# Weight loads that convert, bfloat16 transposes of the gating matrix, x^T by DMA, and work moved from VectorE to GpSimd and ScalarE in a sparse-attention + gMLP kernel

## Chip, cores and metric

The kernel runs on one core of a Trainium2 chip. The metric is device time in microseconds (us), the median of several executions. Engines are named as in the profile: PE (TensorE matmul), PEld (its weight loads), DVE (VectorE), ACT (ScalarE), POOL (GpSimd), SP (SyncE, which here only issues DMAs).

## What is computed

Four batches, 8 heads, 768 positions, head size 64. Attention where each query looks only into the 6 chunks of 32 keys with the highest upper bound of its score; the result, as x (768×512 per batch), goes through a gated feed-forward block whose gate mixes positions with a 768×768 matrix `w_sg`.

```python
ub = sum(maximum(q * k_min_of_chunk, q * k_max_of_chunk))     # per query and chunk
scores = where(chunk among top 6 and causal, q @ k.T / 8, -1e9)
x = softmax(scores) @ v
u, vv = split(gelu(x @ w_in))                  # w_in 512 x 1024
v_n = (vv - mean(vv)) / sqrt(var(vv) + 1e-6) * g_ln
out = x + (u * (w_sg @ v_n + b_sg)) @ w_out    # w_out 512 x 512
```

Everything arrives and leaves in float32; the matmuls run in bfloat16 except the transposes of q and k and the bound.

## The kernel before

The 32 (batch, head) combinations are handled as 16 pairs of heads, two heads side by side on the 128 partitions; pairs 4b to 4b+3 make batch b. For a pair:

- `loads` and `load_v` bring k, q and v (rows of 64 float32) into one of three buffers each;
- `kside` transposes k on PE in float32 in two halves, takes minimum and maximum of each chunk on DVE (`W`, L519), copies k^T to `KA` in bfloat16, and subtracts the minima from the maxima (L538: the bound is q·min + relu(q)·(max − min));
- `qside` transposes q, evicts it to `qT`, makes relu(q) = `rT` (L556) and casts q to `QA` on POOL (L560); `vside` casts v to `vx` on POOL (L570);
- `select` (pairs 0 to 3) or `select_full` (two pairs together) forms the bounds on PE (L595, L642), transposes them on DVE, finds the sixth largest with MAX8, and makes the 0/1 mask `Dt`; from pair 4 on it is copied by DMA into spare rows of `QA`, so that the mask is added by the score matmul itself;
- `scores` / `scores_full` make scores (L750 and L756, or L710), ACT takes the exponential into `E` (L765, L716; two buffers, so pair p waits until pair p−2 has used its own), and POOL zeroes the upper triangle of the diagonal blocks (L721, L772);
- `head` does attention·V (L788, and L795 for the diagonal blocks), divides by the sum (L803, L805) and puts x into `XS`.

When a pair is done, `xtrans` transposes its 128 columns of x (one block, 128×768) on PE into `xT` (L817) and ACT evicts it (L420, called by `evac`). After four pairs `moe_h` computes the v half (L832), gelu and mean and variance on ACT and DVE (L836, L841, L843), the reciprocal root on POOL (L847), the normalised `vhat` on DVE (L859), then the u half (L870, L875). `moe_g` multiplies `w_sg^T` with `vhat` (L887), scales and gates on DVE (L893, L897), multiplies with `w_out` (L906), adds x (L913) and stores (L917; three buffers `osb`).

The weights are loaded once, by SP, in float32 into places that are free early (`vgb`, `osb`, `xT`, `uT`, `vhat`). POOL casts `w_in` and `w_out` to bfloat16 (`cast`, L416). `w_sg` is transposed on PE in float32, three blocks of 128 columns at a time (L457), and evicted to `wsgT` in bfloat16 by DVE (L423).

The program is a list of operations with their dependences; the order on each engine and the buffer of each PSUM tile come from a table found by a search outside the kernel (`TABLE`). Each engine runs its list strictly in order and waits on semaphores. SP's list is its DMA queue: an entry that waits holds everything behind it. A few warm-up matmuls ("filler", L362) are placed on PE at the start. A class of POOL and ACT operations that move data to other partitions is kept in order on POOL (`shift`).

Of the kernel before, what the change touches and what calls it, by code (L numbers as in the profile page):

```python
# [44 lines left out]
class Program:  # L45
# [215 lines left out]
def _build(nc, ctx, q, k, v, w_in, g_ln, w_sg, b_sg, w_out, out):  # L261
    B, H, S, DH = q.shape
    DM = H * DH
# [50 lines left out]
    KBIG = 16  # L314
    VHACT = ()
# [5 lines left out]
    VACT = 16  # L321
    KDVE = (2,)
    QDVE = (2, 3)
    QACT = 16
    WEV = "dve"
# [3 lines left out]
    vn = [T(f"vn{i}", [128, NT, 2, DH], F32) for i in range(NQS)]  # L329
# [57 lines left out]
    P.op("dve", lambda d: d.tensor_tensor(INDF[:], IND[:, 0], IND[:, 1], op=ALU.add), dve(S, rate=2), ("init", 13),  # L387
         port=True, reads=["IND"] + [("IND", n) for n in range(3)], writes=["INDF"])
# [37 lines left out]
    vgA = vgb[:].rearrange("p a b -> p (a b)")  # L426
    xT1 = xT[1][:].rearrange("p a b -> p (a b)").bitcast(F32)
    uT1 = uT[1][:].rearrange("p a b -> p (a b)").bitcast(F32)
    vh1 = vhat[1][:].rearrange("p a b -> p (a b)").bitcast(F32)
    xT1n = [("xT", 1, dk) for dk in range(NDK)]  # L430
    uT1n = [("uT", 1, fb, tg) for fb in range(NF) for tg in range(2)]
    vh1n = [("vhat", 1, qt) for qt in range(NT)]

    def win_load(i):
        dst = vgA[:, DFF * i:DFF * i + DFF] if i < 3 else xT1[:, 0:DFF]
        names = [("vg", 2 * i), ("vg", 2 * i + 1)] if i < 3 else xT1n
        load(dst, bass.AP(w_in.tensor, 128 * DFF * i, [[DFF, 128], [1, DFF]]), ("wi", i), names, 1700)
        cast(winb[:, i, :], dst, DFF, ("wic", i), names, [("winb", i)])

    def wout_load(j):  # L440
        dst = osb[j][:] if j < 3 else xT1[:, DFF:DFF + DM]
        names = [("osb", j)] if j < 3 else xT1n
        load(dst, bass.AP(w_out.tensor, 128 * DM * j, [[DM, 128], [1, DM]]), ("wo", j), names, 900)
        cast(woutb[:, j, :], dst, DM, ("woc", j), names, [("woutb", j)])

    def wsg_load(j):
        base, names = ((uT1, uT1n), (vh1, vh1n))[j % 4 // 2]
        k2 = j % 2
        dst = base[:, S * k2:S * k2 + S]
        load(dst, bass.AP(w_sg.tensor, 128 * S * j, [[S, 128], [1, S]]), ("ws", j), [("stg", j % 4)], 1350)  # L450
        for hf in range(2):
            t = ps_g.tile((0, 1))

            def tr(e, t=t, dst=dst, hf=hf):
                for x in range(3):
                    c = TG * hf + 128 * x
                    r = e.matmul(t.ap()[:, 128 * x:128 * x + 128], dst[:, c:c + 128], identF[:], is_transpose=True)  # L457
                return r
            P.op("pe", tr, pe32(*[128] * 3), ("wst", j, hf), reads=[("stg", j % 4)] + names + ["identF"], writes=[t],
                 alloc=t)  # L460
            evac(WEV, lambda j=j, hf=hf: wsgT[:, 3 * hf:3 * hf + 3, 128 * j:128 * j + 128],
                 lambda t=t: t.ap()[:, 0:TG].rearrange("p (j x) -> p j x", x=128), TG, ("wev", j, hf), [t],
                 [("wsgT", j, hf)], [t], 1)
# [16 lines left out]
    def load_v(p):  # L480
        s = p % NQS
        for i in range(2):
            P.op("sp", lambda e, i=i: e.dma_start(
                vn[s][:, :, i, :], bass.AP(v.tensor, (2 * p + i) * S * DH,
                                           [[DH, 128], [128 * DH, NT], [1, DH]])), dmac(),
                ("vn", p, i), writes=[("vn", s, i)], dma=f"vn{s}_{i}", xfer=940, bulk=NBULK)
# [9 lines left out]
    def kside(p):  # L496
        s, w = p % NQS, p % NW
        if p < KBIG:
            parts = [(hf, hf + 1, ps_g.tile((0, 1, 2, 3) if p < 6 else (0, 1))) for hf in range(2)]
        else:  # L500
            parts = [(0, 2, [ps_g.tile((x,)) for x in range(2)])]
        for h0, h1, t in parts:
            ts = t if h1 - h0 == 2 else [t]
# [27 lines left out]
        if p >= KSPR:  # L531
# [6 lines left out]
        P.op("dve", lambda d: d.tensor_tensor(W[w][:, 1, 0:NC], W[w][:, 1, 0:NC], W[w][:, 0, 0:NC],  # L538
                                              op=ALU.subtract), dve(24), ("wsub", p), port=True, reads=ws, writes=ws)

    def qside(p):
        s, w, r = p % NQS, p % NW, p % NR
        for hf in range(2):
# [5 lines left out]
            if p >= QACT:  # L549
                for i in range(2) if p >= HALF else (None,):  # L550
                    r0, r1 = (0, 128) if i is None else (64 * i, 64 * i + 64)
                    P.op("act", lambda e, t=t, hf=hf, i=i, r0=r0, r1=r1: e.activation(
                        QA[w][i or 0][r0:r1, TG * hf:TG * hf + TG], t.ap()[r0:r1, 0:TG], ACTF.Copy),
                        act(TG), ("qcast", p), reads=[t], writes=[("QA", w, i or 0, hf)], ps=[t])
        qk = [("qT", r, 0), ("qT", r, 1)]
        P.op("dve", lambda d: d.tensor_scalar(rT[r][:], qT[r][:, LO:S], 0.0, None, op0=ALU.max),  # L556
             dve(NSEL, rate=2), ("rel", p), port=True, reads=qk, writes=[("rT", r)])
        for i in () if p >= QACT else range(2) if p >= HALF else (None,):
# [4 lines left out]
    def vside(p):  # L563
        s, w = p % NQS, p % NW
        rd = [("vn", s, 0), ("vn", s, 1)]
        if p >= VACT:
            P.op("act", lambda e: e.activation(vx[w][:, :, :, 0:DH], vn[s][:], ACTF.Copy), act(S), ("vcast", p),
                 reads=rd, writes=[("vx", w)])
        else:
            P.op("pool", lambda g: g.tensor_copy(vx[w][:, :, :, 0:DH], vn[s][:]), gps(S), ("vcast", p),  # L570
                 reads=rd, writes=[("vx", w)])
# [238 lines left out]
    def xtrans(b, dk):  # L810
        src = XS[:, b % 2, dk]
        rd = [("XS", b % 2, 2 * dk), ("XS", b % 2, 2 * dk + 1)]
        t = ps_g.tile((0, 1))
# [9 lines left out]
    def moe_h(b):  # L823
# [25 lines left out]
        if b in VHACT:  # L849
            P.op("dve", lambda d: d.scalar_tensor_tensor(nmr[s][:], mv[s][:, :, 0], -1.0, rstd[s][:], op0=ALU.mult,  # L850
                                                         op1=ALU.mult), (80, 155), ("nmr", b), port=True,
                 reads=[("rstd", s)] + [("mv", s, qt) for qt in range(NT)], writes=[("nmr", s)])
            for qt in range(NT):
                P.op("act", lambda e, qt=qt: e.activation(vhat[s][:, qt, :], vg[qt], ACTF.Identity,
                                                          bias=nmr[s][:, qt:qt + 1], scale=rstd[s][:, qt:qt + 1]),
                     (F / 1.2 + 110, F / 1.2 + 210), ("vhat", b, qt),
                     reads=[("vg", qt), ("nmr", s), ("rstd", s)], writes=[("vhat", s, qt)])
        for qt in range(NT) if b not in VHACT else ():
            P.op("dve", lambda d, qt=qt: d.tensor_scalar(vhat[s][:, qt, :], vg[qt], mv[s][:, qt, 0:1],  # L859
                                                         rstd[s][:, qt:qt + 1], op0=ALU.subtract,  # L860
                                                         op1=ALU.mult),
                 (456, 548), ("vhat", b, qt), port=True, reads=[("vg", qt), ("mv", s, qt), ("rstd", s)],
                 writes=[("vhat", s, qt)])
# [15 lines left out]
    def moe_g(b):  # L879
        s = b % 2  # L880
        for tg in range(2):
            for fb in range(NF):
                t = ps_g.tile((2, 3) if b < B - 1 else None)

                def pt(e, t=t, fb=fb, tg=tg):
                    for sb in range(NT):
# [4 lines left out]
                     reads=[("vhat", s, j) for j in range(NT)] + [("wsgT", j, hf) for j in range(3 * tg, 3 * tg + 3) for hf in range(2)],  # L891
# [72 lines left out]
    for p in range(4, NP + 4):  # L964
# [152 lines left out]
```

## Time and profile before

| | |
|---|---|
| median of 3 runs | 222.42 us (221.57 to 222.50) |
| span of the profiled execution, first to last instruction | 219.6 us |
| granted clock of TensorE | 1.000 |
| DMA: mean rate over the span | 158 GB/s, 34.71 MB in 84508 packets |

For the profiled execution the record gives its span; the runs' times are those of other executions and include what lies around the span. A row of a group of instructions reads: line, engine, operation, output<-input, shapes, count | busy time in us, mean ns of one | idle time of the engine just before them and what ended it. A row of the chain of waits reads: start, duration, engine, output, line, count. That chain is followed back from the last instruction, at each step to what released it.

### The profile page before, as it was taken

Reading aid. Unit: us, or ns where it says so; the run is one execution under the profiler, and the core shown is the slowest. Engines: PE = TensorE matmul, PEld = TensorE weight load, DVE = VectorE, ACT = ScalarE, POOL = GpSimd, SP = SyncE. Lnnn points to the kernel's source line nnn. Section 1 sums busy time; section 2 is a strip of 40 time slices with the busy share of each in tenths; the row PEclk is TensorE's granted clock in tenths of the full one; section 3 lists DMA queues with packets and bytes.
Section 4 is the critical chain, followed back from the end, with each engine's and each line's share of the span. In section 5 each row is a group of like instructions: output and inputs, shape, how many; then the busy total and the mean of one; then the engine's idle time right before and its main releaser. Section 6 shows DMA issues by size and latency. Waiting matters only on the chain.

```text
span 219.6 us, 6004 instructions
## 1 busy us (share of the span) xinstructions
PE 207.9 (95%) x2357; PEld 137.9 (63%) x2373; DVE 189.7 (86%) x545; ACT 163.2 (74%) x247; POOL 84.6 (39%) x112
## 2 busy tenths in 40 slices
PE   7889899989999999998999999999999999999992
PEld 3556667754776578696556686879645669455540
DVE  4899995799999999995999998998798776698993
ACT  3766999795698577999869789799977979654000
POOL 8214748940525736366251073664202133011000
PEclk9999999999999999999999999999999999999999
DMA  7999999989779998996999719333201001003116
GB/s 154 218 219 216 254 280 219 297 223 218 154 210 243 243 258 223 216 261 170 222 218 204 145 50 217 107 106 105 56 1 27 3 34 65 3 0 137 54 53 238
DMA packets 84508, 34.71 MB, mean 158 GB/s; under 512 B 77184, under 2 KB 79488, under 8 KB 84480
## 3 DMA queue, kind: packets, MB, share of 16 engines
q1 hardware_dynamic: 84480, 34.32, 67.9%
q8 instruction: 19, 0.31, 0.6%
q14 instruction: 9, 0.07, 0.1%
HBM read 24.77 MB, written 6.29 MB: 141 GB/s over the span
## 4 chain that ended last, share of the span: by engine, by line
PE 69%; DVE 19%; ACT 9%; issue 2%; DMA 1%; DVEq 0%
PE PSG L887 12%; PE PSC L710 12%; PE PSG L832 9%; PE PSG L906 8%; PE PSG L870 7%; PE PSG L491 6%; ACT E L765 6%; PE PSG L788 5%; DVE W L519 4%; DVE rT L556 3%; PE PSG L642 3%; PE PSG L795 2%; PE PSG L817 2%; PE PSC L362 2%; DVE PSG L893 1%
## 5 line engine op out<-in xcount | busy, mean ns | idle before, releaser
L716 ACT ACTIVATE E<-PSC 128x1024 bf16<-128x1024 f32 (+1 forms) x72 | 62.9, 921 | 9.8 <-PE PSC L710 9.4
L519 DVE TENSOR_REDUCE W<-PSG 128x12 f32<-128x384 f32 x64 | 32.8, 546 | 6.0 <-PE PSG L491 5.7
L710 PE MATMUL PSC<-QA,KA 128*128 128x128 bf16 (+2 forms) x336 | 36.9, 246 | 0.0
L560 POOL CAST QA<-qT 64x768 bf16<-64x768 f32 (+1 forms) x28 | 23.8, 850 | 30.0 <-ACT qT L420 22.1
L887 PE MATMUL PSG<-wsgT,vhat 128*128 128x384 bf16 x192 | 34.9, 326 | 0.3 <-DVE U L657 0.2
L721 POOL TENSOR_SCALAR_AFFINE_SELECT E<-E 128x768 bf16<-128x768 bf16 x24 | 20.8, 865 | 35.7 <-ACT E L716 35.5
L710 PEld LDWEIGHTS PSC<-QA,KA 128*128 128x128 bf16 x336 | 24.5, 98 | 8.3 <-ACT E L716 1.5
L875 ACT ACTIVATE uT<-PSG 128x384 bf16<-128x384 f32 x32 | 15.7, 491 | 17.4 <-PE PSG L870 17.0
L887 PEld LDWEIGHTS PSG<-wsgT,vhat 128*128 128x128 bf16 x192 | 17.7, 98 | 12.5 <-DVE uT L897 1.2
L870 PE MATMUL PSG<-xT,winb 128*128 128x384 bf16 x128 | 24.0, 326 | 0.0
L765 ACT ACTIVATE E<-PSC 128x1024 bf16<-128x1024 f32 (+1 forms) x24 | 20.7, 921 | 2.8 <-PE PSC L756 2.6
L906 PE MATMUL PSG<-woutb,uT 128*128 128x512 bf16 x86 | 21.7, 379 | 0.6
L832 PE MATMUL PSG<-winb,xT 128*128 128x512 bf16 x91 | 21.3, 379 | 0.7 <-ACT vgb L836 0.2
L893 DVE SCALAR_TENSOR_TENSOR PSG<-PSG,glnT,bsgbc 128x384 f32<-128x384 f32 x32 | 19.6, 619 | 2.6 <-PE PSG L887 2.1
L570 POOL CAST vx<-vn 128x768 bf16<-128x768 f32 x16 | 13.3, 829 | 17.8 <-DMA vn<-in_v_dram 13.5
L420 ACT ACTIVATE KA<-PSG 128x384 bf16<-128x384 f32 (+1 forms) x38 | 18.1, 488 | 2.6 <-DVE W L519 2.5
L788 PE MATMUL PSG<-vx,E 128*128 128x65 bf16 x480 | 19.7, 193 | 0.3 <-DVE rden L803 0.3
L788 PEld LDWEIGHTS PSG<-vx,E 128*128 128x128 bf16 x480 | 17.6, 98 | 1.6 <-DVE XS L805 0.4
L913 DVE TENSOR_TENSOR osb<-PSG,XS 128x512 f32<-128x512 f32 x24 | 16.1, 682 | 2.7 <-PE PSG L906 1.3
L805 DVE TENSOR_TENSOR XS<-PSG,rden 128x384 bf16<-128x384 f32 x32 | 17.7, 554 | 0.8
L897 DVE TENSOR_TENSOR uT<-PSG,uT 128x384 bf16<-128x384 f32 x32 | 17.5, 555 | 0.9
L836 ACT ACTIVATE vgb<-PSG 128x512 f32<-128x512 f32 x24 | 13.9, 597 | 5.8 <-PE PSG L832 5.7
(84 smaller groups left out, 347.4 us busy)
## 6 DMA issues: line engine op xcount, KB each, us to landing
kn<-in_k_dram SPq DMA_DIRECT2D x32, 192.0 KB, 4.4
qn<-in_q_dram SPq DMA_DIRECT2D x32, 192.0 KB, 4.5
vn<-in_v_dram SPq DMA_DIRECT2D x32, 192.0 KB, 4.6
out_dram<-osb SPq DMA_DIRECT2D x24, 256.0 KB, 2.3
uT<-in_moe_w_sg_dram SPq DMA_DIRECT2D x4, 384.0 KB, 5.0
KA<-INDF SPq DMA_DIRECT2D x16, 96.0 KB, 4.1
vgb<-in_moe_w_in_dram SPq DMA_DIRECT2D x3, 512.0 KB, 6.4
QA<-Dt SPq DMA_DIRECT2D x24, 36.0 KB, 1.9
```

What stands on the lines that cost most here:

```text
L519: P.op("dve", lambda d, m=m, op=op, src=src, h0=h0, h1=h1: d.tensor_reduce(W[w][:, m, 12 * h0:12 * h1].rearrange("p (h c) -> p h c", h=h1 ...
L560: P.op("pool", lambda g, i=i, r0=r0, r1=r1: g.tensor_copy(QA[w][i or 0][r0:r1, :], qT[r][r0:r1, :]), gps(S, 250 if i == 1 else 150), ("qca ...
L710: r = e.matmul(t.ap()[:, o:o + n], KA[w][i][:, 128 * kb:128 * kb + 128], QA[w][i][:, q0:q0 + n], start=True, stop=True)
L716: P.op("act", lambda e, t=t, c0=c0, c1=c1, i=i: e.activation(E[es][:, i, c0:c1], t.ap()[:, 0:c1 - c0], ACTF.Exp, scale=SCALE), act(c1 - c0 ...
L721: P.op("pool", lambda g, ev=ev: g.affine_select(ev, ev, pattern=[[0, NT], [1, 128]], compare_op=ALU.is_ge, fill=0.0, base=0, channel_multi ...
L765: P.op("act", lambda e, t=t, c0=c0, c1=c1, n=n: e.activation(E[es][:, :, c0:c1], t.ap().rearrange("p (i x) -> p i x", i=2)[:, :, 0:n], ACT ...
L788: r = e.matmul(t.ap()[:, 65 * qb:65 * qb + 65], E[es][:, i, a:a + 128], vx[w][:, kb, i, :], start=first, stop=False, skip_group_check=True)
L832: r = e.matmul(t.ap()[:, 0:F], xT[s][:, dk, 128 * qt:128 * qt + 128], winb[:, dk, F:DFF], start=(dk == 0), stop=(dk == NDK - 1))
L870: r = e.matmul(t.ap()[:, 0:TG], winb[:, dk, 128 * fb:128 * fb + 128], xT[s][:, dk, TG * tg:TG * tg + TG], start=(dk == 0), stop=(dk == NDK ...
L887: r = e.matmul(t.ap()[:, 0:TG], vhat[s][:, sb, 128 * fb:128 * fb + 128], wsgT[:, sb, TG * tg:TG * tg + TG], start=(sb == 0), stop=(sb == N ...
L893: P.op("dve", lambda d, t=t, fb=fb, tg=tg: d.scalar_tensor_tensor(t.ap()[:, 0:TG], t.ap()[:, 0:TG], glnT[:, fb:fb + 1], bsgbc[:, TG * tg:T ...
L906: r = e.matmul(t.ap()[:, 0:DM], gT[s][:, fb, 128 * qt:128 * qt + 128], woutb[:, fb, :], start=(fb == 0), stop=(fb == NF - 1))
```

## The change

- `w_in`, `w_out` and `w_sg` are loaded by DMAs that POOL issues and that convert float32 to bfloat16 on the way (`gload`). The POOL casts of `w_in` and `w_out` are gone; the loads go straight into `winb` and `woutb`. There are 14: 4, 4 and 6.
- `w_sg` is transposed in bfloat16, six blocks of 128 columns per tile and one eviction of 768 columns per tile (before: float32, three blocks, 384 columns).
- `rT` (16 times), the subtraction in `W` (16 times) and the one addition that makes `INDF` go from DVE to POOL.
- x^T: the blocks (2,0), (2,1), (2,2), (2,3), (3,0), (3,1) (batch, block; from 0) are transposed by a DMA that SP issues, without PE, PSUM and ACT's eviction.
- `vhat` of batches 1 and 2 (counted from 0; the second and third) is computed on ACT as vg × rstd + (−mean × rstd); −mean and its product with rstd are two small POOL operations.
- The two loads of v per pair become one; `vn` has another layout.
- `TABLE` is new: all orders, all PSUM slots, and the fillers (9, 1, 2 and 2 instead of 7, 3, 3 and 3). The POOL memsets of the zero rows of `QA`, first in POOL's list before, come later.

```diff
-        pool = self.order["pool"]
+        pool = [i for i in self.order["pool"] if ops[i].dma is None]
...
+    VH = ("dve","act","act","dve")
+    XDMA = ((2, 0), (2, 1), (2, 2), (2, 3), (3, 0), (3, 1))
...
-    P.op("dve", lambda d: d.tensor_tensor(INDF[:], IND[:, 0], IND[:, 1], op=ALU.add), dve(S, rate=2), ("init", 13),
+    P.op("pool", lambda g: g.tensor_tensor(INDF[:], IND[:, 0], IND[:, 1], op=ALU.add), (800, 850), ("init", 13),
...
+    def gload(dst, src, tag, names, xfer):
+        P.op("pool", lambda e: e.dma_start(dst, src), (GP, GP), tag, writes=names, dma="_".join(str(x) for x in tag),
+             xfer=xfer)
+
     def win_load(i):
-        load(dst, bass.AP(w_in.tensor, 128 * DFF * i, [[DFF, 128], [1, DFF]]), ("wi", i), names, 1700)
-        cast(winb[:, i, :], dst, DFF, ("wic", i), names, [("winb", i)])
+        gload(winb[:, i, :], bass.AP(w_in.tensor, 128 * DFF * i, [[DFF, 128], [1, DFF]]), ("wi", i), [("winb", i)], 1650)
...
     def wsg_load(j):
+        gload(stg, bass.AP(w_sg.tensor, 128 * S * j, [[S, 128], [1, S]]), ("ws", j), [("stg", j)], 1250)
...
-                    r = e.matmul(t.ap()[:, 128 * x:128 * x + 128], dst[:, c:c + 128], identF[:], is_transpose=True)
+                for x in range(NT):
+                    r = e.matmul(t.ap(BF16)[:, 128 * x:128 * x + 128], stg[:, 128 * x:128 * x + 128], identB[:], is_transpose=True)
...
-        P.op("dve", lambda d: d.tensor_tensor(W[w][:, 1, 0:NC], W[w][:, 1, 0:NC], W[w][:, 0, 0:NC],
-                                              op=ALU.subtract), dve(24), ("wsub", p), port=True, reads=ws, writes=ws)
+        P.op(WSUB, lambda d: d.tensor_tensor(W[w][:, 1, 0:NC], W[w][:, 1, 0:NC], W[w][:, 0, 0:NC],
...
+        if REL == "pool":
+            P.op("pool", lambda g: g.tensor_scalar(rT[r][:], qT[r][:, LO:S], 3.4028234e38, 0.0, op0=ALU.min, op1=ALU.max),
+                 (640, 690), ("rel", p), reads=qk, writes=[("rT", r)])
...
     def xtrans(b, dk):
+        if (b, dk) in XDMA:
+            P.op("sp", lambda e: e.dma_start(xT[b % 2][:, dk, :].rearrange("p (j x) -> p j x", x=128),
+                                             src.rearrange("p j x -> p (j x)"), transpose=True), dmac(TRI),
+                 ("xtr", b, dk), reads=rd, writes=[("xT", b % 2, dk)], dma=f"tr{b}_{dk}", xfer=TRX)
+            return
...
+        if VH[b] != "dve":
+            P.op("pool", lambda g: g.tensor_scalar(nmr[s][:], mv[s][:, :, 0], -1.0, 0.0, op0=ALU.mult, op1=ALU.add),
+                 (190, 240), ("nmr", b), reads=[("mv", s, qt) for qt in range(NT)], writes=[("nmr", s)])
+        if VH[b] == "act":
+            P.op("pool", lambda g: g.tensor_tensor(nmr[s][:], nmr[s][:], rstd[s][:], op=ALU.mult), (182, 238), ("nmr2", b),
+                 reads=[("nmr", s), ("rstd", s)], writes=[("nmr", s)])
...
+            elif VH[b] == "act":
                 P.op("act", lambda e, qt=qt: e.activation(vhat[s][:, qt, :], vg[qt], ACTF.Identity,
                                                           bias=nmr[s][:, qt:qt + 1], scale=rstd[s][:, qt:qt + 1]),
```

In the new order POOL issues the loads `ws` 0 and 1 between its work for pairs 2 and 3; `wi` 0, `ws` 5, `ws` 3, `wi` 2 and `wi` 3 one after another between the triangular masks of the two heads of pair 1, and `wi` 1 behind the second of them; the other six after pair 5's work has begun. SP issues the x^T transposes (2,1), (2,0), (2,2), (2,3) one after another, then a store and the key copies of pairs 14, 13 and 15; later (3,0) and (3,1).

More of the change, by code (lines that the diff above doesn't have):

```diff
@@ L386, in _build @@
              ("init", 10 + n), reads=["IND"], writes=[("IND", n)])
-    P.op("dve", lambda d: d.tensor_tensor(INDF[:], IND[:, 0], IND[:, 1], op=ALU.add), dve(S, rate=2), ("init", 13),
-         port=True, reads=["IND"] + [("IND", n) for n in range(3)], writes=["INDF"])
+    P.op("pool", lambda d: d.tensor_tensor(INDF[:], IND[:, 0], IND[:, 1], op=ALU.add), (800, 850), ("init", 13),
+         reads=["IND"] + [("IND", n) for n in range(3)], writes=["INDF"])
     INDR = ["IND"] + [("IND", n) for n in range(3)]
@@ L442, in wout_load @@
-        names = [("osb", j)] if j < 3 else xT1n
-        load(dst, bass.AP(w_out.tensor, 128 * DM * j, [[DM, 128], [1, DM]]), ("wo", j), names, 900)
-        cast(woutb[:, j, :], dst, DM, ("woc", j), names, [("woutb", j)])
+        gload(woutb[:, j, :], bass.AP(w_out.tensor, 128 * DM * j, [[DM, 128], [1, DM]]), ("wo", j), [("woutb", j)], 850)
     def wsg_load(j):
[L447 to L450, printed above, removed]
@@ L497, in kside @@
         s, w = p % NQS, p % NW
[L498 to L503, printed above, removed]
+        for h0, h1, t in [(hf, hf + 1, ps_g.tile((0, 1, 2, 3) if p < 6 else (0, 1))) for hf in range(2)]:
+            ts = [t]
             def tr(e, h0=h0, ts=ts):
@@ L854, in moe_h @@
                 P.op("act", lambda e, qt=qt: e.activation(vhat[s][:, qt, :], vg[qt], ACTF.Identity,
                                                           bias=nmr[s][:, qt:qt + 1], scale=rstd[s][:, qt:qt + 1]),
-                     (F / 1.2 + 110, F / 1.2 + 210), ("vhat", b, qt),
+                     (F / 1.2 + 85, F / 1.2 + 185), ("vhat", b, qt),
                      reads=[("vg", qt), ("nmr", s), ("rstd", s)], writes=[("vhat", s, qt)])
[L858 to L863, printed above, removed]
+            else:
+                P.op("dve", lambda d, qt=qt: d.tensor_scalar(vhat[s][:, qt, :], vg[qt], mv[s][:, qt, 0:1],
+                                                             rstd[s][:, qt:qt + 1], op0=ALU.subtract,
+                                                             op1=ALU.mult),
+                     (456, 548), ("vhat", b, qt), port=True, reads=[("vg", qt), ("mv", s, qt), ("rstd", s)],
+                     writes=[("vhat", s, qt)])
@@ L890, in moe_g @@
                 P.op("pe", pt, pe(*[TG] * NT), ("pt", b, tg, fb),
-                     reads=[("vhat", s, j) for j in range(NT)] + [("wsgT", j, hf) for j in range(3 * tg, 3 * tg + 3) for hf in range(2)],
+                     reads=[("vhat", s, j) for j in range(NT)] + [("wsgT", j) for j in range(3 * tg, 3 * tg + 3)],
                      writes=[t], alloc=t)
```

97 lines of the change are left out of this document (43 added, 54 removed), and 115 rows, old and new, of the table TABLE.

## The prediction

> **What bounds the kernel now.** I read the page's first part, then the busy time by stage, cut where the chain of waits changes its engine: at 50.2 us (first matmul of the feed-forward part) and 213.15 us (last wait on TensorE).
>
> ```profile
> span 219.6 us, 6004 instructions
> PE 207.9 (95%) x2357; PEld 137.9 (63%) x2373; DVE 189.7 (86%) x545; ACT 163.2 (74%) x247; POOL 84.6 (39%) x112
> ```
>
> ```profile
> 0.00:50.20 50.20, 44.66 (x660) 30.11 (x663) 41.46 (x126) 39.04 (x58) 28.91 (x48) 1.00 1.05 231
> 50.20:213.15 162.95, 160.68 (x1692) 106.82 (x1702) 145.48 (x416) 124.16 (x189) 55.67 (x64) 1.00 0.57 132
> 213.15:219.60 6.45, 2.55 (x12) 0.98 (x10) 2.77 (x4) 0.00 (x0) 0.00 (x0) 1.00 0.66 245
> ```
>
> The columns are PE, PEld, DVE, ACT and POOL busy time, the granted clock, the DMA share and GB/s. In the middle stage PE is busy for all but 162.95 − 160.68 = 2.3 us: there time is bought by taking work from PE, and little by relieving anyone else. The first stage is different; the chain of waits shows on whom it runs:
>
> ```profile
> 8.32 0.47 DVE INDF L387
> 8.79 0.99 DVE rT L556
> 14.35 0.72 DVE rT L556
> 21.22 0.81 DVE W L538
> 24.26 1.94 ACT E L765 x2
> 36.74 3.93 ACT E L765 x5
> 41.08 1.18 DVE rT L556
> 46.02 0.81 DVE W L538
> 47.30 0.70 DVE rT L556
> 50.23 1.19 PE PSG L832 x5
> 85.31 0.46 PE PSG L788 x15
> 119.81 0.66 PE PSG L491 x6
> 124.44 0.88 PE PSC L710 x11
> 155.37 1.13 PE PSG L642 x32
> 185.09 0.67 PE PSG L817 x12
> 194.69 0.86 PE PSG L906 x4
> 213.15 0.70 DVE osb L913
> ```
>
> It runs on DVE to about 24 us, on ACT (the exponentials) to 41 us and on DVE again to 49 us. The tail is the last six sums, their three buffers and their stores; the change leaves its order alike, so I keep its 6.45 us. The span is 219.6 us and the median of the runs 222.42, so 2.8 us lie around the span; I take off what the span loses.
>
> **PE work.** A float32 transpose of 128 columns costs 0.66 / 6 = 0.110 us back to back, a bfloat16 one 0.67 / 12 = 0.056 us.
>
> ```profile
> 0.00:50.20 50.20, 4.06 (x24) 2.51 (x24) 1.00 1.05 231
> 50.20:213.15 162.95, 1.97 (x12) 1.56 (x12) 1.00 0.57 132
> ```
>
> These are the w_sg transposes (L457) in the first two stages. All 36 become bfloat16; the 12 in the middle stage save 12 × 0.054 = 0.65 us there, and the 24 in the first stage 1.3 us that PE, not the bound there, does not need. Six x^T blocks leave PE: 36 transposes × 0.056 = 2.0 us, all of batches 2 and 3 and so in the middle stage. Together −2.65 us. Of the 2.3 us of gaps I let a third (0.8 us) go, because the engine that PE waits for is mostly DVE and DVE loses work; the ends are 0 and 2.3.
>
> **DVE work.**
>
> ```profile
> L556 DVE TENSOR_SCALAR rT<-qT x16: 437/453/1177, 8.7 to 144.4; 128x576 f32<-128x576 f32 x16
> L538 DVE TENSOR_TENSOR W<-W x16: 166/180/883, 8.1 to 153.4; 128x24 f32<-128x24 f32 x16
> L556 DVE TENSOR_SCALAR rT<-qT 128x576 f32<-128x576 f32 x16 | 10.1, 644 | 0.1
> L538 DVE TENSOR_TENSOR W<-W 128x24 f32<-128x24 f32 x16 | 4.2, 266 | 0.2
> L859 DVE TENSOR_SCALAR vhat<-vgb,mv,rstd 128x512 bf16<-128x512 f32 x24 | 11.3, 539 | 1.0 <-POOL rstd L847 1.0
> L423 DVE CAST wsgT<-PSG 128x384 bf16<-128x384 f32 x12 | 6.5, 547 | 0.3 <-PE PSG L457 0.2
> L420 ACT ACTIVATE xT<-PSG x16: 803/814/904, 35.9 to 187.8; 128x768 bf16<-128x768 bf16 x16
> L836 ACT ACTIVATE vgb<-PSG 128x512 f32<-128x512 f32 x24 | 13.9, 597 | 5.8 <-PE PSG L832 5.7
> ```
>
> DVE gives 10.1 us (rT) and 4.2 us (W) to POOL, half of 11.3 us (vhat) to ACT, and replaces twelve 0.547 us evictions by six of 768 bfloat16 columns. No row has that eviction on DVE; between 0.45 us and the 0.81 us that ACT takes for this size I take 0.65 (nearest in rate to DVE's 384 columns in 0.547 if a packed type helps somewhat): 6.5 − 3.9 = 2.6 us. In all some 23 us of 189.7.
>
> On the chain of the first stage the pieces above that leave DVE are 0.47 + 0.99 + 0.72 + 0.81 + 1.18 + 0.81 + 0.70 = 5.7 us. But rT is then made by POOL on the same path (query eviction, rT, bound matmul), four times on this chain.
>
> ```profile
> L570 POOL CAST vx<-vn 128x768 bf16<-128x768 f32 x16 | 13.3, 829 | 17.8 <-DMA vn<-in_v_dram 13.5
> L381 POOL TENSOR_SCALAR_AFFINE_SELECT IND<-IND 32x768 bf16<-32x768 bf16 x2 | 1.6, 818 | 0.1
> L416 POOL CAST winb<-vgb 128x1024 bf16<-128x1024 f32 x3 | 3.4, 1119 | 2.6 <-DMA vgb<-in_moe_w_in_dram 2.6
> L412 SPq DMA_DIRECT2D vgb<-in_moe_w_in_dram x3: 432/543/780, 26.7 to 36.1; - x3
> L474 SPq DMA_DIRECT2D kn<-in_k_dram x32: 373/652/1723, 0.8 to 131.5; - x32
> ```
>
> By elements, 829 × 576 / 768 = 622 ns, so 0.65 us each: 2.6 us come back and the first stage gains 5.7 − 2.6 = 3.1 us. The ends: 0, if ACT's chain from 24 to 41 us swallows it, and 41.46 − 39.04 + 3.1 = 5.5 us, if DVE's relief counts down to ACT's load and beyond it as far as the chain does. INDF (about 0.8 us on POOL) is late by that much for the first mask row copies only, which stand far down SP's queue.
>
> **POOL work.** The eight weight casts go (L416: 1.1 us for the large, in all about 7.5 us), rT (10.4), W (about 3) and INDF come, and 14 weight loads are issued here. No row shows an issue on POOL; SP's for the same loads take 0.43 to 0.78 us, its longest of all 1.72 us. I take 0.8 us, with 0.43 and 1.72 as ends. In the first stage eight loads precede the feed-forward part: 28.91 − 4.4 (four casts) + 5 × 0.65 (rT) + 5 × 0.2 (W) + 0.8 + 8 × 0.8 = 36 us, below ACT's 39. So the issues cost nothing on average; the cover is POOL's idle time, and where it fails is the place with five of them in a row, between the two triangular masks of pair 1: the second mask, its attention·V product and the E buffer that pair 3 fills are queued behind. At 0.8 us that is 4 us where POOL now has none; pair 3's exponentials begin at 36.7 us, which covers it.
>
> **ACT work.** It loses six x^T evictions (6 × 0.81 = 4.9 us) and gains 12 normalisations; the nearest row, 128×512 from PSUM, says 0.60 us: 7.2 us. Each batch's six take 3.6 us where DVE's took 2.8 (11.3 / 4), and the mean times rstd is one more POOL step: up to 1 us later for batches 1 and 2. The first of them waits for POOL's power, and behind it in ACT's queue stand the gelu evictions whose PSUM buffers PE's next u blocks need. PE has interleaved scores there; I count 0, with +2 as the far end.
>
> **x^T by DMA.** Nothing in the trace transposes in a DMA. SP issues six; the fourth, (2,3), waits for the last head of pair 11, and behind it wait a store, the key copies of pairs 13 to 15 and pair 14's and 15's selection rows. In the new PE order there lie between that head and batch 2's first feed-forward matmul, by the chain's rows: three score chunks of 0.44 us (0.88 for two) and two of 640 columns (0.28), three key transposes (0.33), one output block (0.86), two attention·V products of 21 matmuls (0.46 × 21 / 15 = 0.64) and one bound matmul group (1.13): 5.5 us. Needed: 0.75 us (reciprocal and scaling) plus issue and landing.
>
> ```profile
> kn<-in_k_dram SPq DMA_DIRECT2D x32, 192.0 KB, 4.4
> KA<-KA SPq DMA_DIRECT2D x8, 96.0 KB, 3.8
> DMA to landing us min/median/max: 2.2/3.8/5.2
> ```
>
> The last line is KA's. An x^T block is 192 KB: 4.4 us as a load, 10.4 us at twice the slowest on-chip copy. I take the load's size, since DMA is nearly idle then: 0.75 + 4.4 is hidden by 5.5. The far end is 5.6 us late.
>
> Sum: −3.1 − 2.65 − 0.8 = −6.5 us: span 213.1, time 215.9, say 216.0.
>
> The Trainium skill, VectorE: DVE Perf Modes, section "The three transpose paths", gives 1309 ns for a 128×128 block by DMA against 390 ns on TensorE, and advises TensorE where the result may go to PSUM. By that figure, six blocks one after another would be an estimated 7.9 us, and the time about 219; the trace's 0.056 us per block on PE (back to back) shows the same side cheaper, but PE is what is short here.
>
> **The rivals.**
> A. Only PE's work counts: POOL returns in the first stage what DVE gives. For it: POOL is in order and holds long casts. 222.4 − 2.65 = 219.8.
> B. The first stage shrinks to the far end (5.5) and all gaps close (2.3): 222.4 − 5.5 − 2.65 − 2.3 = 212. For it: outside ACT's stretch nearly all of the first stage's chain is DVE. Against it: ACT's unbroken chain from 24 to 41 us.
> C. The transposes land late, by 5.6 us at batch 2: 216.0 + 5.6 = 221.6.
> D. Slower: POOL bounds the first stage. The largest times of L556 and L538 (1.18 and 0.88 us against medians of 0.45 and 0.18) are DVE instructions held up beside POOL; POOL may be held up as long. With those maxima and 1.72 us per issue POOL's load is 28.91 − 4.4 + 5 × 1.18 + 5 × 0.88 + 0.8 + 8 × 1.72 = 49.4 us; with the 8.7 us that DVE, the bound now, still idled, 58.1 instead of 50.2. Then +7.9 − 2.65 − 0.8 = +4.5: 226.9. It decides from a load of 50.2 − 8.7 + 3.45 = 45 us on. Against it: the instructions that met in those maxima no longer run on DVE.
> The Trainium skill, SBUF — State Buffer, section "SBUF: two separate sides", says that a load issued from GpSimd cannot get its descriptors written while VectorE runs an instruction in a two-port mode; that speaks for D. The maxima of L556 and L538 agree that the two engines hold each other up; no run here shows it for an issue.
>
> **How the numbers follow.** Forecast 0.48 (its own range 212.5 to 219), A 0.12, B 0.14, C 0.10, D 0.16. Half a per cent, 1.1 us, is about what a measurement of this kernel tells from no change. C lies inside it (0.07 there, 0.03 faster); D's weaker forms put 0.01 there. Faster 0.48 + 0.12 + 0.14 + 0.03, less 0.03 for a forecast that fails by small stalls: 0.74; same 0.08; slower 0.18. The range 209.5 to 225 takes in B, A, C and part of D.
>
> **What would show it.** In the profile after: the first L832 matmul of batch 0 near 47 us (right) or after 50 (A, D); POOL's issues at 0.4 to 0.8 us or far longer; rT near 0.65 us; PE without a wait on xT before batch 2; DVE near 167 us busy, POOL near 106, ACT near 165. PE waiting on rT, on W or on a mask in the first 50 us, or on a weight load, would make the prediction wrong.

## The result and the profile after

The changed kernel takes 229.4 us (median of 4 runs, 228.88 to 230.22) against 222.46 (221.57 to 222.83) for the kernel before on the same chip: ratio 1.032, 95% interval 1.029 to 1.036. It is slower, and the forecast was 216.0. Medians here are over all executions of a kernel; ratios leave out those that took over 1.5% longer than its fastest.

The page of the changed kernel, its first lines, and the busy time by stage, cut where the chain reaches the v matmuls (55.12 us) and at the last wait on TensorE (222.5). The columns are those of the prediction.

```profile
span 228.5 us, 5907 instructions
PE 208.8 (91%) x2335; PEld 134.4 (59%) x2335; DVE 169.9 (74%) x494; ACT 167.1 (73%) x253; POOL 98.7 (43%) x155
```

```profile
0.00:55.12 55.12, 44.73 (x656) 30.00 (x657) 32.67 (x108) 37.50 (x57) 34.08 (x64) 0.94 1.01 184
55.12:222.50 167.38, 161.29 (x1668) 103.32 (x1666) 135.14 (x384) 129.57 (x197) 64.58 (x91) 1.00 0.59 131
222.50:228.50 6.00, 2.76 (x12) 1.09 (x12) 2.07 (x3) 0.00 (x0) 0.00 (x0) 1.00 0.47 175
```

The work moved as meant: DVE 20 us less, POOL 14 more, ACT 4 more. But the first stage is 4.9 us longer than before (50.20), the middle one 4.4 (162.95), where PE now idles 167.38 − 161.29 = 6.1 us instead of 2.3. The first stage's clock is 0.94.

The mark at 50.20 us needs care. The prediction calls it the first matmul of the feed-forward part; PE's own list in the kernel before shows that batch 0's v matmuls begin at 46.19 us with a group of four (three on record) and go on at 50.16 with the other twenty (nineteen on record):

```profile
46.19 0.81 PE L832 MATMUL PSG<-winb,xT 128*128 128x512 bf16 x3
50.16 4.49 PE L832 MATMUL PSG<-winb,xT 128*128 128x512 bf16 x19
```

Where orders differ I therefore compare the end of all 24: 54.7 us before, 61.1 in the changed kernel. The chain of waits of the changed kernel says where the time is lost:

```profile
28.95 13.40 DMA vn<-in_v_dram
42.35 0.05 issue
42.40 0.85 POOL vx L557
43.25 0.14 issue
43.38 0.98 PE PSG L775 x15
```

The v load of pair 2 takes 13.4 us; PE waits for its cast. In slices of 2 us (columns: PE, PEld, DVE, ACT, POOL busy, granted clock, DMA share, GB/s):

```profile
36.00:38.00 2.00, 0.86 (x11) 0.41 (x5) 0.00 (x0) 2.00 (x4) 0.00 (x0) 1.00 1.15 206
38.00:40.00 2.00, 0.00 (x0) 0.00 (x0) 0.00 (x0) 0.97 (x2) 0.00 (x0) 1.00 1.13 205
40.00:42.00 2.00, 0.00 (x0) 0.00 (x0) 0.00 (x0) 0.00 (x0) 0.00 (x0) 0.69 1.06 216
42.00:44.00 2.00, 0.61 (x12) 0.65 (x13) 0.00 (x0) 0.00 (x0) 1.54 (x3) 0.50 0.76 175
44.00:46.00 2.00, 2.00 (x24) 1.63 (x23) 0.57 (x3) 0.00 (x0) 1.74 (x4) 0.50 1.17 255
46.00:48.00 2.00, 2.00 (x35) 1.37 (x30) 0.52 (x2) 1.02 (x1) 2.00 (x4) 0.60 1.20 209
48.00:50.00 2.00, 1.44 (x38) 1.17 (x37) 1.22 (x3) 1.95 (x4) 1.68 (x3) 1.00 0.62 109
```

From about 37 to 42.4 us no engine but ACT works, and from 39 us not even ACT, while DMA is full; then PE, from 43.4 to nearly 48, runs at half its clock. What fills DMA is seen by queue in 35 to 40 us (packets, MB, share of 16 engines), beside the issues on POOL:

```profile
q0 software_dynamic: 544, 0.90, 96.7%
q1 hardware_dynamic: 486, 0.12, 17.8%
```

```profile
L436 POOL DMA_DIRECT2D winb<-in_moe_w_in_dram x4: 556/562/575, 29.3 to 32.8; - x4
```

q0 carries POOL's converting loads, q1 SP's. The packets go nearly one for one, but POOL's hold 0.90 MB / 544 = 1.65 KB and take 0.967 × 16 × 5 us / 544 = 142 ns, SP's hold 256 bytes and take 29 ns. A v load of 384 KB is 1536 packets, 96 for each of 16 engines; at 142 + 29 ns a turn that is an estimated 16 us, and 13.4 were seen. The estimate is rough: the two shares add up to 114%, so these times overlap, and the turns do not fill the whole wait. They are plainest from 36 to 38 us (217 and 210 packets) and from 38 to 40 (194 and 194).

The other rows to compare with the prediction: the normalisation on ACT, and the x^T transposes on SP.

```profile
L854 ACT ACTIVATE vhat<-vgb,nmr,rstd x12: 797/804/815, 119.0 to 176.5; 128x512 bf16<-128x512 f32 x12
```

```profile
L801 SPq DMA_TRANSPOSE xT<-XS x6: 1209/1302/2227, 153.0 to 191.0; - x6
...
DMA to landing us min/median/max: 2.8/3.1/4.3
```

The normalisations cost 0.80 us each. Among PE's waits none names a transposed x^T block.

### The profile page after: what moved, and what is told of

The parts are those of the page before. It is cut to its first block, busy times and chain, and to the rows that moved or that the text cites. A ratio compares the mean times of both kernels' runs of the same rounds, so it can differ in the third digit from the quotient of the medians.

```text
span 228.5 us, 5907 instructions
## 1 busy us (share of the span) xinstructions
PE 208.8 (91%) x2335; PEld 134.4 (59%) x2335; DVE 169.9 (74%) x494; ACT 167.1 (73%) x253; POOL 98.7 (43%) x155
## 4 chain that ended last, share of the span: by engine, by line
PE 66%; ACT 16%; DMA 8%; DVE 5%; issue 1%; POOL 1%; SPq 1%; DVEq 0%
PE PSG L887 14%; PE PSC L697 9%; PE PSG L906 8%; PE PSG L824 8%; PE PSG L488 7%; DMA vn<-in_v_dram 6%; PE PSG L775 5%; PE PSG L870 4%; ACT vhat L854 4%; ACT uT L875 2%; ACT KA L424 2%; DMA qn<-in_q_dram 2%; DVE W L512 2%; PE PSG L629 2%; PE PSC L366 2%; ACT E L752 2%
## 5 line engine op out<-in xcount | busy, mean ns | idle before, releaser
L697 PE MATMUL PSC<-QA,KA 128*128 128x128 bf16 (+2 forms) x336 | 37.5, 246 | 0.0
L875 ACT ACTIVATE uT<-PSG 128x384 bf16<-128x384 f32 x32 | 15.1, 485 | 19.2 <-PE PSG L870 19.1
L775 PE MATMUL PSG<-vx,E 128*128 128x65 bf16 x480 | 20.7, 197 | 8.7 <-POOL vx L557 6.5
L906 PE MATMUL PSG<-woutb,uT 128*128 128x512 bf16 x96 | 24.0, 380 | 1.2 <-DVE uT L897 1.2
L552 POOL CAST QA<-qT 64x768 bf16<-64x768 f32 (+1 forms) x28 | 23.2, 830 | 1.2
L824 PE MATMUL PSG<-winb,xT 128*128 128x512 bf16 x96 | 22.7, 380 | 0.1
L790 DVE RECIPROCAL rden<-PSG 128x6 f32<-128x6 f32 x32 | 6.0, 189 | 19.9 <-PE PSG L782 19.8
L833 DVE BATCH_NORM_STATS2 stats<-vgb 128x6 f32<-128x512 f32 x24 | 16.2, 686 | 2.8 <-ACT vgb L828 2.3
```

What stands on the lines that cost most here:

```text
L552: P.op("pool", lambda g, i=i, r0=r0, r1=r1: g.tensor_copy(QA[w][i or 0][r0:r1, :], qT[r][r0:r1, :]), gps(S, 250 if i == 1 else 150), ("qca ...
L697: r = e.matmul(t.ap()[:, o:o + n], KA[w][i][:, 128 * kb:128 * kb + 128], QA[w][i][:, q0:q0 + n], start=True, stop=True)
L775: r = e.matmul(t.ap()[:, 65 * qb:65 * qb + 65], E[es][:, i, a:a + 128], vx[w][:, kb, i, :], start=first, stop=False, skip_group_check=True)
L824: r = e.matmul(t.ap()[:, 0:F], xT[s][:, dk, 128 * qt:128 * qt + 128], winb[:, dk, F:DFF], start=(dk == 0), stop=(dk == NDK - 1))
L906: r = e.matmul(t.ap()[:, 0:DM], gT[s][:, fb, 128 * qt:128 * qt + 128], woutb[:, fb, :], start=(fb == 0), stop=(fb == NF - 1))
```

## Experiments

Ratios are to the kernel before, run beside each on the same chip, with 95% intervals. Orders are given as moves in an engine's list.

**The late loads.** SP's and POOL's orders in the first stage, one at a time:

```diff
 SP (e1)
+vn2 vn3
 mask-row copy of pair 1 (waits for its scores)
 qn5 kn5
-vn2 vn3
```

> Changed kernel, SP's list only: the v loads of pairs 2 and 3 stand ahead of the mask-row copy that waits for pair 1's scores (they were issued at 29 us, behind it). Theory of turns (each converting weight packet is large and takes one turn against one small packet of SP's queue, so loads issued during the weights starve): v of pair 2 lands before 34 us instead of 42.4, PE's pause from 36 to 43 us and the half clock after it go, time 222 to 224 (from 229.4). Rival (the v load is only the first of several late things, the key and query loads and mask rows are next): the pause shrinks by under 3 us, time above 226.5.

228.87 us, 1.031 (1.026 to 1.037): no gain. The v loads land in time, and PE waits all the same:

```profile
38.33 0.55 PE PSG L488 x3
38.91 0.50 ACT qT L424
39.41 4.17 issue
43.58 0.87 PE PSG L488 x3
```

The 4.17 us end with a key transpose, and the key load issued at 28.8 us took 14.7 us to land, up to 43.5. The wait moved from v to k, as the rival said.

```diff
 POOL (e2)
-wi0 ws5 ws3 wi2 wi3 ... wi1          (among the masks of pair 1)
 v cast of pair 2
+wi0 wi1 wi2 wi3 ws3 ws5
```

> Changed kernel, POOL's list only: the four w_in loads and w_sg blocks 3 and 5 are issued behind the cast of v of pair 2 instead of between the masks of pair 1. Theory of turns: v of pair 2, with nothing beside it, lands in about 6 us (about 35 us instead of 42.4), and the weights then have until 47 us: time 222 to 225. Rival (the bytes have to come through before the feed-forward part whatever the order): the wait moves from v to w_in in front of the first feed-forward matmul, which then starts no earlier than the 55 us of now: time 228 to 231.

226.76 us, 1.023 (1.019 to 1.027): some 2 us better than the changed kernel, but the burst now holds up what SP issues from 37 us on, and PE is idle for 3.2 of the 4 us from 40 us on. Both edits together, with less in the burst:

```diff
 SP (e5):   vn2 vn3 and the last qn5, kn5 ahead of the mask-row copy of pair 1
 POOL (e5): wi0 wi1 wi2 wi3 behind the v cast of pair 2; ws3 ws5 behind rT of pair 5
 PE (e5):   transposes of ws3, ws5 behind the six v matmul groups of batch 0
 DVE (e5):  the evictions of these transposes among batch 0's statistics
```

> The changed kernel with both queues reordered in the first stage: on SP the v loads of pairs 2 and 3 and the last q and k loads of pair 5 stand ahead of the mask-row copy that waits for pair 1's scores; on POOL the four w_in loads stand behind the v cast of pair 2 and two w_sg loads behind pair 5's rT, with their transposes behind the first v matmuls. Theory (the converting loads take turns with SP's and what PE needs next arrives late, so PE idles 5 us and then runs 8 us at a half clock): with v ahead and the burst behind, nothing that PE needs is in the burst; first feed-forward matmul at 49 to 51 us instead of 55.1, granted clock 1.0 throughout, median 222 to 225. Rival (the load queues are full whatever the order, the wait only moves to the next load): PE idles at another place before 50 us, first feed-forward matmul at 53 or later, median 226 to 229.

223.52 us, 1.0055 (1.0025 to 1.0086): 5.9 us better than the changed kernel. The stage of e5 up to its first v matmul, and what follows:

```profile
0.00:46.40 46.40, 41.43 (x643) 27.25 (x643) 31.79 (x106) 36.82 (x56) 33.89 (x64) 1.00 1.06 194
46.40:214.98 168.58, 162.47 (x1689) 103.97 (x1681) 136.22 (x385) 130.15 (x198) 65.01 (x92) 1.00 0.62 137
```

The clock stays at 1.00 in both stages, the twenty v matmuls start at 46.6 us, and all 24 are done at 52.8. Of the change nothing is taken out; only its order is another. Is the converting load harmless by itself? The kernel before with the weights' part alone (with it the bfloat16 transposes of w_sg, v in one load a pair, and INDF on POOL), the loads spread as SP had issued them:

> The kernel before with the weights' part of the change alone: converting loads on POOL, each at the place in POOL's queue that its issue on SP has by time in before (so spread over 18 to 70 us, no more than two in a row), the casts gone, w_sg transposed in bfloat16, v loaded by one DMA a pair; rT, normalisation and x^T as before, INDF on POOL. Theory (only the burst of six loads in 4 us starves SP's; the converting load itself costs nothing): 220 to 222.3. Rival (large converting packets delay SP's 256-byte ones wherever they stand): 224 or more, with PE idle between 25 and 50 us.

221.75 us, 0.9999 (0.9976 to 1.0022). Harmless when spread out: what cost was the burst.

**The normalisation on ACT.** First the kernel before with that part alone:

```diff
-    VHACT = ()
+    VHACT = (1, 2)
```

> The kernel before with one part alone: the normalisations of batches 1 and 2 on ScalarE (0.80 us each by the changed kernel's trace against 0.47 on DVE), placed among the gelu evictions as the changed kernel has them. Theory (ScalarE is the busier engine there and the attention-free gap behind u has no cover): PE loses about 1 to 2 us per batch, median 224 to 226. Rival (scores cover it): 222 to 223.

227.72 us, 1.025 (1.019 to 1.031): 5.6 us for an edit that was counted at nothing. PE's waits from 100 us on in e7 (engine, line, releaser: us in total, times, longest); the kernel before has none above 0.3 there:

```profile
PE PSG L870 <- ACT uT L875: 2.9, 2, 1.6
PE PSG L887 <- ACT uT L875: 1.7, 2, 1.4
PE PSG L788 <- ACT uT L875: 1.4, 1, 1.4
```

These 6.0 us are waits for gelu evictions (uT) that stand behind normalisations in ACT's list; the price holds for the places in that list that I gave them. In the changed order the same move back was tried three times:

```diff
-    VH = ("dve","act","act","dve")
+    VH = ("dve","dve","dve","dve")
 DVE (e3):      batch 1's six behind the whole transposes of pair 10, batch 2's behind the first maxima of pair 14
 DVE (e10, e9): batch 1's ahead of those transposes, batch 2's behind all those maxima
 e9 is e5 with this edit; e3 and e10 are the changed kernel with it
```

> Changed kernel with the normalisations of batches 1 and 2 back on DVE, in one piece behind the selection's first steps; the two small POOL operations go. Theory that ACT is the late one there (0.80 us for one against 0.51 planned, and gelu evictions behind them): PE's gaps at 120 to 130 us (1.2 us) and 170 to 180 us (2.9 us) go, time 225 to 226.5 (from 229.4). Rival (the gaps come from the statistics and POOL's power, which stay): 228.5 to 230.

232.5 us, 1.039 (1.031 to 1.047), an interval that overlaps the changed kernel's (1.029 to 1.036): no gain.

> The changed kernel with only the normalisations of batches 1 and 2 back on DVE, at the places of e9; its loads are left as they are. If the two causes add up, this gains on the changed kernel what e9 gains on e5_loads_first (3 to 5.5 us): median 224 to 226.5. If the late loads hide the rest (PE's lost time in the first stage sets the end and the later waits only follow from it), it gains under 1.5 us: 228 to 229.5.

229.21 us, 1.031 (1.024 to 1.039): no gain.

> e5_loads_first with the normalisations of batches 1 and 2 back on DVE, in stretches where that run's DVE was idle: batch 1's six behind the bound reductions of pair 10 (idle from 110.1 to 113.2 us there), batch 2's behind the maxima of pair 14 (idle from 164.4 to 167.1). Theory (the normalisations delay the gelu evictions behind them in ScalarE's queue, and through their PSUM buffers PE's u blocks): the six waits of PE on uT, 2.8 us there, and what hangs on them go; the kernel before lost 5.6 us by the same move, so this gains 3 to 5.5 us on 223.5: median 218 to 220.5, below the kernel before. Rival (DVE's queue passes the delay on to the mask of pairs 10 and 14): 222 to 225.

222.33 us, 1.0036 (1.0003 to 1.007): 1.2 us better than e5 in the medians, 0.4 by the ratios, which compare each with the kernel before on its own chip, and the intervals overlap. A gain is not shown. In the changed order DVE passes on most of what ACT had cost: PE waits 1.8 us for XS and 1.1 for U instead.

**x^T by DMA.** Taken out of the changed kernel, and put alone into the kernel before (blocks (2,0) to (2,2) and (3,0) to (3,2)):

```diff
-    XDMA = ((2, 0), (2, 1), (2, 2), (2, 3), (3, 0), (3, 1))
+    XDMA = ()
```

> Changed kernel with all x^T blocks on PE again and ACT's six evictions with them. Theory that the transposing DMAs do what was meant (landing in 3.1 us, hidden): PE's 2.0 us come back, time 231 to 232. Rival (SP is held up to 2.2 us by each and everything behind it is late, or ACT was relieved where it did not matter): no change or a gain, 228 to 229.5.

236.24 us, 1.066 (1.060 to 1.072). PE waits 3.8 us in all for the evictions of these blocks in ACT's list, at the places that I chose for them. So this run prices that order, and not the blocks.

> The kernel before with one part of the change alone: six x^T blocks, three of batch 2 and three of batch 3, by transposing DMA on SP; everything else as before. Theory (PE's work counts one for one in the middle stage, and the landing is hidden): 36 matmuls of 0.056 us less on PE, median 219.5 to 220.5, and a change of 0.988 or so. Rival (PE's place is taken by another wait, or SP's queue holds up what stands behind): 222 to 225. The run of the changed kernel with the blocks back on PE cost 6.8 us; if that were the blocks' worth and not the order around them, this run would come out near 216.

221.77 us, 0.998 (0.995 to 1.002): no change that can be measured. Its middle stage:

```profile
50.00:213.00 163.00, 159.63 (x1666) 105.09 (x1665) 145.88 (x416) 120.15 (x183) 55.42 (x64) 1.00 0.62 139
```

The cuts are round numbers; the twenty v matmuls start at 49.8 and the last wait on TensorE is at 212.9, so the stage is as long as before (162.95). PE is busy 1.05 us less in it than before (160.68), and its gaps grew from 2.3 to 3.4 us by what its work lost. (The trace of before has 2357 PE records where e8, with the same PE list, has 2373, so its busy time may read a few tenths low.)

**rT, W and INDF on POOL,** alone in the kernel before, and together with x^T:

> The kernel before with one part alone: rT, W's subtraction and INDF on POOL instead of DVE, at the places in POOL's queue that their times on DVE in the trace of before give; weights loaded and cast as before. By the prediction's first term the first stage would shorten by 3.1 us if POOL's own queue does not hold them up: median 219 to 221. Rival (POOL is in order and DVE's pieces were not what set the stage, or the longer POOL form returns them): 222 to 224.

221.29 us, 0.997 (0.994 to 1.001). Its chain of waits:

```profile
34.85 5.16 DMA xT<-in_moe_w_in_dram
...
45.07 1.02 PE PSG L832 x4
...
48.75 4.42 PE PSG L832 x20
...
60.25 4.37 DMA KA<-INDF
```

PE's list is that of the kernel before, so its rows compare directly with the two shown above for that kernel:

```profile
45.07 1.02 PE L832 MATMUL PSG<-winb,xT 128*128 128x512 bf16 x4 [0.70 <-POOL winb L416]
48.68 4.49 PE L832 MATMUL PSG<-winb,xT 128*128 128x512 bf16 x20
```

The first four v matmuls wait 0.7 us for the cast of a w_in load and come 1.1 us earlier than before, the other twenty 1.5 us earlier; DMA holds 12% of the chain, 1% in the kernel before.

> The kernel before with two parts of the change together, those of e8_before_pool_rT (rT, W's subtraction and INDF on POOL) and of e6_before_xT_dma (six x^T blocks by DMA), in the order of before. Alone they came to 0.9973 and 0.9982 of before. If the two gains add up: 220.8 to 221.4. If the x^T blocks' PE work counts only where the rest no longer waits: 219.5 to 220.5. If the queues pass each other's delays on: 222 or more.

220.74 us, 0.9949 (0.9921 to 0.9976): 1.1 us faster than the kernel before, a small gain that is clear of the noise.

**Where the gain of the first stage goes.** These runs looked for 5 us, the distance from e8's first v matmuls to the mark at 50.2; by the rows above only 1.1 to 1.5 us were there to be found. First, other work laid over the chain from v matmul to pt, then loads ahead of SP's waits:

```diff
 PE (e11):  two score chunks of pair 13 among batch 2's v matmuls; its second attention-value product behind the u blocks
 DVE (e11): transposes of pair 10 between batch 1's third and fourth normalisation
 SP (e12):  e11, and kn6 gln bsg qn8 qn9 qn9 vn4 ahead of pair 4's selection rows; kn10 vn6 qn11 vn7 qn11 ahead of batch 0's first store
```

> e9_loads_first_dve_norm with other work put between the value matmuls and the pt matmuls of batch 2, as the order of before has it (two score chunks of pair 13 among its v matmuls, pair 13's second attention-value product behind its u blocks instead of ahead of the last two), and on DVE three of batch 1's normalisations behind pair 10's transposes instead of ahead of them. e9's trace shows PE losing 2.5 us in 160 to 170 and 1.5 us in 110 to 120, at the chain v matmul, statistics, power, normalisation, pt; before loses 0.45 and 0.28 us there. Theory (what is left of the loss lies in the new order on PE, which has less independent work over that chain): 2 to 3 us come back, median 219.5 to 220.5, below the kernel before. Rival (the wait moves to another place, since the chain's length sets it): 221.5 to 223.

222.33 us, 1.0028 (1.0002 to 1.0055): as e9. PE's waits moved on to uT and qT.

> e11_cover and, on SP, loads moved ahead of two copies that wait: seven ahead of the first selection row copy of pair 4 (SP waited 6.5 us there from 48 us, at which time DMA moved 52 GB/s in the changed kernel and 183 before), five ahead of batch 0's first output store (5.4 us from 74). Theory (the later stretch 90 to 100, where e9 loses 1.7 us of PE to q loads that land late, is SP's order): 1 to 1.7 us less than e11_cover. Rival (the loads are no earlier because their queue is full, or pair 4's rows come later for them): equal to e11_cover within 0.7 us, or slower.

233.41 us, 1.045 (1.037 to 1.052). The seven loads delay the selection rows, and PE idles into the lower clock again:

```profile
60.00:64.00 4.00, 1.01 (x7) 0.62 (x8) 1.94 (x5) 1.20 (x3) 0.00 (x0) 0.97 0.62 141
64.00:68.00 4.00, 4.00 (x27) 3.06 (x25) 0.30 (x1) 1.95 (x4) 0.00 (x0) 0.60 0.33 74
```

Then five sixths of the v loads of pairs 4 to 9 were left out in three kernels: the one before (e13), e8 (e14) and e11 (e15). Shown is the load's shape:

```diff
-    [[DH, 128], [128 * DH, NT], [1, DH]]
+    [[DH, 128], [128 * DH, 1 if 4 <= p <= 9 else NT], [1, DH]]
```

> The kernel before with a sixth of the v loads of pairs 4 to 9 (one of six blocks of each head; the rest of each buffer keeps older values): 1.9 MB of the 11 MB loaded between 50 and 110 us left out, 8 us of DMA time at 231 GB/s. Control for the next two. Before, PE lacks little there, so both theories expect 221 to 222.3.

221.91 us, 1.0017 (0.9976 to 1.0059).

> e8_before_pool_rT with the same loads left out. That kernel has its first v matmul at 45.1 us and its sixth at about 53, against 50.2 and 54.5 before, but ends at the same time, and its chain of waits has DMA and SP's queue in it between 57 and 112 us. Theory (the loads set the pace up to some 115 us: DMA share is 0.9 to 1.1 in before up to 120 us, so time won in the first stage is waited for again): with less to load the gain of the first stage reaches the end, median 218.5 to 220, 1.5 to 3 us below e13_before_less_v. Rival (the gain was PE work moved past the first v matmul, nothing to do with DMA): equal to e13 within 1 us.

220.12 us, 0.996 (0.992 to 1.000): 1.8 us below e13 in the medians, as the theory has it, but e8 had a gain of its own, and e14's interval overlaps e8's and e13's.

> e11_cover with the same loads left out. If loads set the pace, its loss of 1.3 us of PE in 90 to 100 goes: 220 to 221.2. If not, 222 to 222.6. Either way what it loses at the normalisations of batches 1 and 2 stays.

221.80 us, 1.0025 (0.9989 to 1.006): no gain, so in this order the loads of that stretch are not what is missing.

```diff
+        z = 1 - s if b in (1, 2) else s
-    vhat[s][:, qt, :], vg[qt], mv[s][:, qt, 0:1], rstd[s][:, qt:qt + 1]
+    vhat[s][:, qt, :], vg[qt], mv[z][:, qt, 0:1], rstd[z][:, qt:qt + 1]
```

> e11_cover where the normalisations of batches 1 and 2 read the statistics of the batch before (so the values differ, the instructions and their number do not), each placed on DVE behind its own row block's statistics: the wait for six blocks' statistics and POOL's power is taken out of the chain. Theory (the chain v matmul, statistics, power, normalisation, pt is longer than the work that PE has over it in the new order): PE's losses in 110 to 120 and 160 to 180 (4 us) fall below 1.5, median 219 to 220.5. Rival (PE waits there for PSUM buffers that the gelu evictions free, or for selection rows): 221.5 to 222.5.

224.57 us, 1.016 (1.005 to 1.027), slower, and it decides nothing: the early normalisations hold up the chunk bounds on DVE, ACT's key eviction waits 2.4 us for these, and PE 2.6 us for the gelu behind it.

## Why the prediction was wrong

**What failed first** is the step "POOL work". It counted the 14 loads as time on POOL's queue ("the issues cost nothing on average; the cover is POOL's idle time") and looked for what stands behind them there. As far as it went, that was right: an issue takes 0.56 us (0.8 foreseen), and up to the late v load the chain has no piece on POOL's queue. What is late stands on SP's queue: while the burst lasts, its 256-byte packets go one for one with the large ones. The contention of the loads for the DMA engines was put at nothing. The prediction quoted the row that should have warned it, a DMA share of 1.05 in the first stage, and used only PE to POOL of it. Reordering the loads (e5) gives back 5.9 of the 13.4 us between forecast and result. The prediction would have taken a wait for rT, W, a mask or a weight load as its refutation; the wait came for v. None of the rivals had it; D was right that the first stage lengthens and wrong about why, since POOL's 34.08 us there are below the 36 foreseen. The Trainium skill, DMA: Bandwidth & Descriptors, section "Queues, rings and completion order", says that a DMA engine takes turns between its queues packet by packet; the 544 and 486 packets agree. There a packet is several descriptors; whether the profile's packets are these, no run here shows.

**The first stage's DVE term** (−3.1 us) was the second step that failed: it was mis-sized, and its sign of being right, the first v matmul near 47 us, could not tell: the kernel before already has it at 46.2. Done alone (e8, same PE list) it brings the v matmuls 1.1 to 1.5 us forward and 0.6 us at the end, with an interval that includes no gain. The term added up pieces of the chain as if time went with them, but PE was at work for 44.66 of the 50.20 us, and in the whole kernel before it waits for rT only 1.8 us. In e5 all 24 v matmuls are done 1.8 us earlier than before; up to there PE has 1.3 us less work, since the w_sg transposes are cheaper and partly later, and 0.5 us less idle time. POOL's prices were near: rT 0.67 us (0.65), W 0.24 (0.2); only INDF was off, 1.64 (0.8).

**PE's work** (−2.65 us) was the third: a matmul less in the middle stage was taken as time less, with a further 0.8 us of gaps. In e6 2.0 us of matmuls (0.9% of the time) are gone and the time falls by 0.2%, at most by 0.5%; in e18 the w_sg transposes are cheaper, batch 0's v matmuls are done 1.4 us earlier, and nothing is gained at the end. In e6 the gaps grow by what the work lost. That PE's list had been laid over the other engines' chains, which show when there is less in it, is my reading of this; no run isolates it. Rivals A and B rest on the same step and fall with it.

**ACT's normalisation** was the fourth: 0.80 us each instead of 0.60, and counted at 0 with a far end of 2 us because "PE has interleaved scores there". In the order of before it costs 5.6 us (e7), through the gelu evictions that the prediction itself named as standing behind it. In the changed order, loads mended, moving it back gains 0.4 to 1.2 us, not clearly apart from nothing, so of the changed kernel's loss it explains little.

**Right:** x^T lands in 3.1 us (4.4 foreseen) and nobody waits for it, so rival C is out; DVE 169.9, POOL 98.7 and ACT 167.1 us stand near the 167, 106 and 165 foreseen; the tail is 6.00 us (6.45).

The 13.4 us between forecast and result thus are 5.9 (burst), at most 1.2 (normalisation, not clear of noise), and for the rest, 6.3 us or more, gains that were counted and do not arrive. Done one by one on the order before, rT with W and INDF, x^T, and the weights bring 0.6, 0.4 and 0.0 us, and the first two together 1.1. Why no more arrives stays open: that loads hold back the 1.5 us that e8's first stage wins fits e8's chain and e14's median, but e14's interval does not settle it and e15 speaks against it in the changed order; a shorter chain at the normalisations could not be tested cleanly (e16).

## What to carry to other kernels

Before a load moves to another queue, read the DMA share of the stage: where it is at 1, ask whose packets it will take turns with, and spread large-packet loads out or keep them behind the small-packet loads that the next matmuls need. Where PE is busy 95%, a microsecond of matmuls removed need not be a microsecond gained (e6), and an operation added to ACT is priced by the evictions behind it (e7). Before a stage is cut at "the first matmul" of a part, look that matmul up in the engine's own list: the chain showed only the second group. Try the parts of a change one at a time on the old order: here rT and x^T together gave the only gain clear of the noise, 0.5%.

## What the runs showed of the hardware

- Two queues with work share the engines packet by packet and not by bytes: in 35 to 40 us 544 packets of 1.65 KB and 486 of 256 bytes, 96.7% and 17.8% of the engines' time; from 38 to 40 us 194 and 194.
- The granted clock falls late and comes back late: PE is idle from about 36.9 to 43.3 us; the clock is 1.00 up to about 40.8 us, 0.50 from there, and 1.00 again from about 47.6. So the wait costs an estimated 2 us more (4.2 us of work at half the clock). The Trainium skill, TensorE: Matmul & The Clock Gate, section "What's actually happening", gives a window of about 3.4 us in both directions; the rows, 3.9 us to the fall and 4.3 us to the return, are near it.
- A transposing DMA of 192 KB inside the chip costs SP 1.30 us and lands in 3.1 us; a converting load's issue costs POOL 0.56 us (landing medians of 4.2 to 8.7 us).
